# Decode attention and gated MLP on one core: query and down weights laid out in runs of rows, x loaded from ScalarE's queue

## The chip, the cores and the metric

The kernel runs on one NeuronCore of a Trainium2 chip. The metric is the device time of one execution in microseconds; lower is better. Three runs of the kernel before took 1316.83, 1316.87 and 1317.15 us, so its median is 1316.87 us.

## The reference

One decode step (one new token for each of 4 sequences) of a pre-norm transformer block: attention over a cache of 8192 keys and values for each of 32 heads, then a gated MLP. All inputs are bf16.

```python
B, D, H, Sk, Dh, F = 4, 512, 32, 8192, 128, 1792
def A(x):                                        # x: (4, 1, 512), layer-normed
    q = (x @ wq).reshape(B, 1, H, Dh)            # wq: (512, 4096)
    p = softmax(q . k_cache * Dh**-0.5)          # k_cache: (4, 32, 8192, 128)
    return (p . v_cache).reshape(B, 1, H*Dh) @ wo
def M(x):                                        # layer-normed
    return (sigmoid(x @ w_gate) * (x @ w_up)) @ w_down   # (512,1792), (512,1792), (1792,512)
h  = x + A(layernorm(x))
h2 = h + M(layernorm(h))
```

The two caches are 128 pairs (sequence, head) of 2 MB of keys and 2 MB of values: 537 MB. The weights are 4 MB each for `wq` and `wo` and 1.8 MB each for gate, up and down.

## The kernel before

Work is written out by hand, one list of instructions for each engine (`emit`) and DMAs put in the list of the engine that issues them (`prog.dma`); semaphores order them. All DMAs, x included, are issued by SyncE ("SPq" in the profile), strictly in the order of its list.

**Slots.** SBUF holds a ring of 8 slots of 2 MB (`KV`). Each K head, each V head and each of the three MLP weights takes the next slot (`take_slot`); the DMA that fills it waits until the slot's former holder has been used up. The order of loads is: x (L185), K head 0 in four pieces (L274), `wq` in four pieces of 1 MB (L295, `emit_wq`), K heads 1 and 2, then four pieces of `wo` (L302) between further K heads. From then on K and V heads alternate, V lagging K by 9 heads. `w_gate` stands before the last three V heads; the last V head comes in four pieces; `w_up` (both L290) and `w_down` in two pieces (L285) close the list. The first piece of `wo` overwrites `wq`'s buffer (`Wreg`), so SyncE waits there until the query projection is done.

**Start.** TensorE transposes x by four small matmuls (`f_xT`, L219), VectorE copies the result to `stx` and `sth`, a layer norm follows (`layernorm`, ending in `xnT`). TensorE transposes K head 0 (L360, evictions to `kTc` by ScalarE at L370 and VectorE at L372), then projects the query: 128 matmuls (L533), 32 for each quarter of the 512 rows of `wq`, each quarter waiting for its own DMA. In the stream a matmul loads its second operand into the array as weights (LDWEIGHTS, engine "PEld") and streams the third. Every weight operand of the kernel before is read with consecutive elements.

**Middle.** For each head: 64 transposes of K (L360), 16 score matmuls (L385), softmax for a group of 8 heads, and 16 matmuls with V (L469; for the last group 64 narrow ones a head, L481).

**End.** After the last piece of the last V head: project with `wo` (L498), second layer norm (L194 to L212, ending in `hnT`), gate and up products (L593, `glu_mm`, 56 matmuls each, to PSUM 128 hidden units at a time), sigmoid (L598), product `hhT` (L600), down product (L609, 56 matmuls; 28 for each half of `w_down`, each half waiting for its own DMA), add to the residual (L614), transpose (L616), copy (L618), store (L619).

Which hidden unit lies on which partition is fixed by the loads: before, partition p of tile t holds hidden unit 128 t + p for `w_down`, and `w_gate`/`w_up` columns are taken 128 in a row to match. In the same way partition p of chunk c holds row 128 c + p of `wq`, and `f_xT` puts x's element 128 c + p there.

Of the kernel before, what the change touches and what calls it, by code (L numbers as in the profile page):

```python
# [12 lines left out]
NTB = 4  # L13
NKT = 16
LAGH = 9
GH = 8


class _Prog:
# [27 lines left out]
    def emit(self, eng, fn, waits=(), incs=1):  # L47

        todo = self._waits(eng, waits)
        tok = self.token(eng, incs) if incs else None  # L50

        def run(e):
            for key, v in todo:
                e.wait_ge(self.sems[key], v)
            made = fn(e)
            made = made if isinstance(made, list) else [made]
            if incs:
                assert len(made) == incs
                for m in made:
                    m.then_inc(self.sems[eng], 1)  # L60

        self.ops[eng].append(run)
        return tok
# [14 lines left out]
def bass_sequential_preLN__mha_block_cached__glu_gated_glu__decode_kernel(  # L78
# [12 lines left out]
    B, _sq, D = A_x.shape  # L91
# [3 lines left out]
    NDC = D // 128  # L95
    NFT = F // 128
    R = S // 128
    NK = R // 4
    NH = B * H
    NG = NH // GH  # L100
    SCALE = float(DH) ** -0.5
# [3 lines left out]
    prog = _Prog()  # L105
    emit = prog.emit

    with ExitStack() as es:
        def SB(name, shape, dt):
            return es.enter_context(nc.sbuf_tensor(name, shape, dt))  # L110

        ident = SB("ident", [128, 128], BF16)
        identf = SB("identf", [128, 128], FP32)
        M8 = SB("M8", [128, GH], FP32)
        Gmat = SB("Gmat", [128, 128], FP32)
# [3 lines left out]
        x_bf = SB("x_bf", [B, D], BF16)  # L119
        stx = SB("stx", [128, 2 * NDC * B], FP32)  # L120
        sth = SB("sth", [128, 2 * NDC * B], FP32)
# [4 lines left out]
        q_all = SB("q_all", [128, NH], BF16)  # L126
        Lq = SB("Lq", [128, 2, GH * W], BF16)
        KV = SB("KV", [128, NSL, R * 128], BF16)
        kTc = SB("kTc", [128, NKT, 512], BF16)
        S_sb = SB("S_sb", [128, 512], FP32)  # L130
        E_sb = SB("E_sb", [128, 512], BF16)
        PT = SB("PT", [128, 2, NK * GH * 32], BF16)
        mpart = SB("mpart", [128, 1], FP32)
        mrow = SB("mrow", [1, GH], FP32)
        negmb = SB("negmb", [128, 1], FP32)
        sig = SB("sig", [128, 1], FP32)
        rsum = SB("rsum", [128, 1], FP32)
        O_sb = SB("O_sb", [128, 512], FP32)
        OT = SB("OT", [128, 2, GH], BF16)
        sg_sb = SB("sg_sb", [128, NFT * B], FP32)  # L140
# [5 lines left out]
        Wreg = SB("Wreg", [128, WREG], BF16)  # L146
        wq_v = Wreg[:, :].rearrange("p (c f) -> p c f", c=NDC)
# [7 lines left out]
        def in_slot(slot, inner):  # L155
            return bass.AP(raw(KV), slot * R * 128, [[KVROW, 128], *inner])
# [4 lines left out]
        bank = [PS[:, 512 * i:512 * (i + 1)] for i in range(8)]  # L161
        bankT = bank[0:4]
        SBK, OBK, XS, XO = 4, 5, 6, 7

        keys = ["sp", "act", "dve", "pool", "pe", "x", "out", "wg", "wu", "wd0", "wd1"]
        keys += [f"sl{i}" for i in range(NSL)] + [f"k0p{i}" for i in range(4)] + [f"vl{i}" for i in range(4)]
        keys += [f"wq{i}" for i in range(4)] + [f"wo{i}" for i in range(4)]
        for k in keys:
            prog.sems[k] = es.enter_context(nc.semaphore("s_" + k))

# [3 lines left out]
            out=ident[:, :], in_=ident[:, :], compare_op=ALU.not_equal, fill=1.0, base=0,  # L174
# [3 lines left out]
            out=identf[:, :], in_=identf[:, :], compare_op=ALU.not_equal, fill=1.0, base=0,  # L178
# [3 lines left out]
        t_rp0 = emit("pool", lambda e: e.memset(rowpad[:, :], 0.0))  # L182
        t_pt0 = emit("pool", lambda e: e.memset(PT[:, :, :], 0.0))

        t_x = prog.dma("sp", "x", lambda e: e.dma_start(x_bf[:, :], A_x.rearrange("b s d -> (b s) d")))  # L185


        def cols(t, c):
            return t[:, c:c + NDC * (B - 1) + 1:NDC]
# [26 lines left out]
        def f_xT(e):  # L216
            ins = None
            for c in range(NDC):
                ins = e.matmul(cols(bank[XO], c), x_bf[:, 128 * c:128 * (c + 1)], ident[0:B, 0:B],  # L219
                               start=True, stop=True)  # L220
            return ins
        t_xT = emit("pe", f_xT, [t_x, t_ident])
        t_xTc = emit("dve", lambda e: e.tensor_copy(stx[:, 0:NDC * B], bank[XO][:, 0:NDC * B]), [t_xT])
        t_h = emit("dve", lambda e: e.tensor_copy(sth[:, 0:NDC * B], bank[XO][:, 0:NDC * B]), [t_xT])
        t_xn, t_xst = layernorm(stx, t_xTc, 0, xnT, bank[XS], None)
        t_m8 = emit("dve", lambda e: e.tensor_reduce(
            M8[:, :], identf[:, :].rearrange("p (t i) -> p i t", i=GH), AX.X, ALU.max), [t_identf])
# [11 lines left out]
        t_wq = []  # L239
# [23 lines left out]
        def take_slot(job):  # L263
            i = n_alloc[0] % NSL
            w = freed(held_by[i])
            n_alloc[0] += 1
            held_by[i] = job
            slot_of[job] = i
            return i, w
# [9 lines left out]
        def emit_weight(kind):  # L279
            slot, w = take_slot((kind, 0))  # L280
            if kind == "wd":
                wd_v = in_slot(slot, [[D, NFT], [1, D]])
                src = B_w_down.rearrange("(t p) f -> p t f", p=128)
                half = NFT // 2
                t_w[kind] = (wd_v, [prog.dma("sp", f"wd{i}", lambda e, i=i: e.dma_start(  # L285
                    wd_v[:, half * i:half * (i + 1), :], src[:, half * i:half * (i + 1), :]), w) for i in range(2)])
                return
            view = in_slot(slot, [[F, NDC], [1, F]])
            src = (B_w_gate if kind == "wg" else B_w_up).rearrange("(c p) f -> p c f", p=128)
            t_w[kind] = (view, prog.dma("sp", kind, lambda e: e.dma_start(view, src), w))  # L290

        def emit_wq():
            src = A_wq.rearrange("(c p) f -> p c f", p=128)
            for c in range(NDC):
                t_wq.append(prog.dma("sp", f"wq{c}", lambda e, c=c: e.dma_start(wq_v[:, c, :], src[:, c, :])))  # L295

        t_wo = []
        t_qproj = []
# [7 lines left out]
        for n in range(NH):  # L306
            order.append((4 * n, 0, "k", n))
            order.append((4 * (n + LAGH), 1, "v", n))
        order.sort()
# [218 lines left out]
        def q_projection():  # L528
            for c in range(NDC):
                def f(e, c=c):  # L530
                    ins = None
                    for h in range(H):
                        ins = e.matmul(bank[XO][:, B * h:B * (h + 1)], wq_v[:, c, h * 128:(h + 1) * 128],  # L533
                                       cols(xnT, c), start=(c == 0 and h == 0),
                                       stop=(c == NDC - 1), skip_group_check=True)
                    return ins
                t = emit("pe", f, [t_wq[c], t_xn, t_xTc])
            t_qproj.append(t)
            st_["q"] = st_["xo"] = emit("dve", lambda e: e.tensor_copy(q_all[:, :], bank[XO][:, 0:NH]), [t])
            q_windows(0)  # L540
            q_windows(1)

        def q_windows(g):
            dst = Lq[:, g % 2, 31:31 + W * (GH - 1) + 1:W]
            t_lq[g] = emit("dve", lambda e: e.tensor_copy(dst, q_all[:, GH * g:GH * (g + 1)]),  # L545
                           [st_["q"], t_lq0, t_score.get(32 * (g - 1) - 1)])


        for u in range(4 * (NH + LAGH)):
            n, s = u // 4, u % 4  # L550
# [10 lines left out]
            for su in todo:  # L561
                if su < 4 * NH:
                    scores(su)
                    if su % 32 == 31:
                        if 2 <= su // 32 + 2 < NG:
                            q_windows(su // 32 + 2)
                        for d, fn in softmax(su // 32):
                            chain.append((4 * u + d, fn))
            vu = u - 4 * LAGH
            if vu >= 0:  # L570
# [17 lines left out]
        def glu_mm(wv, bk):  # L588
            def f(e):
                ins = None  # L590
                for t in range(NFT):
                    for c in range(NDC):
                        ins = e.matmul(bk[:, B * t:B * (t + 1)], wv[:, c, 128 * t:128 * (t + 1)],  # L593
                                       cols(hnT, c), start=(c == 0), stop=(c == NDC - 1))
                return ins
            return f
# [3 lines left out]
        t_hh = emit("dve", lambda e: e.tensor_tensor(hhT[:, :], sg_sb[:, :], bank[SBK][:, 0:NF], ALU.mult), [t_sg, t_u])  # L600

        wd_v, t_wd = t_w["wd"]
        half = NFT // 2
        for i in range(2):
            def f_down(e, i=i):
                ins = None
                for t in range(half * i, half * (i + 1)):
                    for c in range(NDC):
                        ins = e.matmul(cols(bank[OBK], c), wd_v[:, t, 128 * c:128 * (c + 1)],  # L609
                                       hhT[:, B * t:B * (t + 1)], start=(t == 0 and c == 0),  # L610
                                       stop=(t == NFT - 1), skip_group_check=True)
                return ins
            t_d = emit("pe", f_down, [t_hh, t_wd[i], t_ot])
# [3 lines left out]
                                            start=True, stop=True), [t_h2])  # L617
# [59 lines left out]
```

## Time and profile before

| | |
|---|---|
| median of 3 runs | 1316.87 us |
| span of the profiled execution (first to last instruction) | 1315.5 us |
| around the span (median less span) | 1.4 us |
| TensorE matmul busy (PE) | 1016.4 us, 77% |
| TensorE weight loads (PEld) | 671.9 us, 51% |
| VectorE (DVE) | 721.1 us, 55% |
| ScalarE (ACT) | 608.7 us, 46% |
| bytes by DMA | 552.68 MB, 420 GB/s over the span |
| mean granted TensorE clock | 0.845 |

The page gives no time of its own for the profiled execution beside its span, so the median of the runs stands in for it. Busy shares are averages over the span; a DMA share of 9 tenths or more means that the 16 DMA engines had packets in flight nearly always. In the chain of waits "SPq" is SyncE issuing DMAs and "DMA" is the time from the end of an issue to the landing. TensorE, where it waits for data, idles "<-DMA".

### The profile page before, as it was taken

The page shows a single profiled execution, that of the slowest core. Times are in us where ns is not written, and L with a number is a line of the kernel's source. Part 1 is how long each engine was busy: PE and PEld are TensorE (multiplying, and loading weights), DVE is VectorE, ACT ScalarE, POOL GpSimd, SP SyncE. Part 2 cuts the span into 40 slices and gives each one's busy share as a digit, 9 for nine tenths or more (in the row PEclk, how much of TensorE's full clock was granted, in tenths as well). Part 3 has the DMA queues.
Part 4 walks back from the last instruction along what each step waited for, and adds up shares of the span by engine and source line. Part 5 has one row for each costly group of instructions (what it writes and reads, how often), then busy time and mean ns, then how long its engine had stood idle before and what let it go on. Part 6 is the DMA issues. An engine that isn't in the chain of part 4 may idle for free.

```text
span 1315.5 us, 29564 instructions
## 1 busy us (share of the span) xinstructions
PE 1016.4 (77%) x13385; PEld 671.9 (51%) x13385; DVE 721.1 (55%) x1210; ACT 608.7 (46%) x1095; POOL 9.0 (1%) x11
## 2 busy tenths in 40 slices
PE   6887877877788787887788778788887878778764
PEld 5654544545455454554455445455554545545443
DVE  5774655556555565555556456555555656556520
ACT  3664544545444454444445445454444545445420
POOL 2000000000000000000000000000000000000000
PEclk8988888888888888788888888888788888888865
DMA  9999999999999999999999999999999999999996
GB/s 381 415 427 426 427 427 427 425 428 425 428 425 426 427 425 428 424 427 426 427 426 426 426 428 424 427 425 428 427 424 426 426 428 425 426 427 428 425 411 245
DMA packets 45510, 552.68 MB, mean 420 GB/s; under 512 B 4420, under 2 KB 10312, under 8 KB 12360
## 3 DMA queue, kind: packets, MB, share of 16 engines
q1 hardware_dynamic: 45384, 550.79, 99.0%
q8 instruction: 105, 1.72, 0.5%
q14 instruction: 21, 0.17, 0.0%
HBM read 550.77 MB, written 0.00 MB: 419 GB/s over the span
## 4 chain that ended last, share of the span: by engine, by line
DMA 81%; PE 16%; SPq 2%; ACT 0%; issue 0%; DVE 0%
DMA KV<-in_A_v_cache_dram 76%; PE PS L360 10%; PE PS L385 3%; PE PS L469 3%; DMA KV<-in_B_w_down_dram 2%; DMA KV<-in_A_k_cache_dram 1%; SPq L277 1%; DMA Wreg<-in_A_wq_dram 1%; SPq L302 0%; SPq L295 0%; ACT kTc L370 0%; SPq L274 0%; ACT L422 0%; PE PS L533 0%; PE PS L481 0%
## 5 line engine op out<-in xcount | busy, mean ns | idle before, releaser
L372 DVE CAST kTc<-PS 128x512 bf16<-128x512 f32 x1024 | 676.1, 692 | 484.4 <-PE PS L360 481.6
L370 ACT ACTIVATE kTc<-PS 128x512 bf16<-128x512 f32 x1024 | 573.4, 595 | 648.2 <-PE PS L360 646.2
L360 PEld LDWEIGHTS PS<-ident,KV 128*128 128x128 bf16 x8192 | 547.5, 109 | 252.3 <-ACT kTc L370 135.7
L360 PE MATMUL PS<-ident,KV 128*128 128x128 bf16 x8192 | 654.7, 240 | 12.8 <-DMA KV<-in_A_k_cache_dram 10.4
L469 PE MATMUL PS<-KV,PT 128*32 128x512 bf16 x1920 | 216.8, 442 | 242.2 <-DMA KV<-in_A_v_cache_dram 242.2
L385 PE MATMUL PS<-kTc,Lq 128*32 128x512 bf16 x2048 | 227.1, 435 | 1.1 <-DVE Lq L545 0.6
L469 PEld LDWEIGHTS PS<-KV,PT 128*32 128x32 bf16 x1920 | 52.4, 99 | 273.9 <-DMA KV<-in_A_v_cache_dram 273.6
L385 PEld LDWEIGHTS PS<-kTc,Lq 128*32 128x32 bf16 x2048 | 53.5, 95 | 64.6 <-issue 19.1
L481 PE MATMUL PS<-PT,KV 128*128 128x1 bf16 x512 | 14.9, 165 | 18.0 <-DMA KV<-in_A_v_cache_dram 15.4
L481 PEld LDWEIGHTS PS<-PT,KV 128*128 128x128 bf16 x512 | 14.3, 104 | 18.6 <-DMA KV<-in_A_v_cache_dram 15.9
L516 PE MATMUL PS<-selq,O_sb 128*128 128x8 f32 x120 | 16.7, 266 | 7.1 <-ACT O_sb L508 7.1
L516 PEld LDWEIGHTS PS<-selq,O_sb 128*128 128x128 f32 x120 | 15.3, 200 | 10.0 <-ACT O_sb L508 10.0
L409 DVE TENSOR_REDUCE mrow<-PS 1x8 f32<-1x128 f32 x16 | 4.5, 279 | 29.2 <-PE PS L405 29.2
L205 ACT ACTIVATE lnw<-lnw 128x4 f32<-128x4 f32 x2 | 0.4, 205 | 38.9 <-DVE lnw L202 38.9
L581 DVE CAST OT<-PS 128x8 bf16<-128x8 f32 x1 | 0.2, 167 | 32.6 <-PE PS L481 32.6
L521 DVE CAST OT<-PS 128x8 bf16<-128x8 f32 x15 | 2.5, 167 | 19.5 <-PE PS L516 19.5
L422 ACT ACTIVATE E_sb<-S_sb,negmb 128x512 bf16<-128x512 f32 x16 | 11.6, 722 | 3.1 <-DVE negmb L420 2.6
L400 DVE TENSOR_REDUCE mpart<-S_sb 128x1 f32<-128x512 f32 x16 | 11.0, 686 | 3.1 <-ACT S_sb L398 1.5
L508 ACT ACTIVATE O_sb<-PS 128x512 f32<-128x512 f32 x15 | 9.0, 597 | 6.3 <-PE PS L469 6.3
L446 DVE CAST PT<-PS 128x512 bf16<-128x512 f32 x16 | 10.9, 682 | 0.7 <-PE PS L438 0.7
L398 ACT ACTIVATE S_sb<-PS 128x512 f32<-128x512 f32 x16 | 9.6, 597 | 1.2 <-PE PS L385 1.1
L405 PE MATMUL PS<-identf,mpart 128*1 128x128 f32 x32 | 7.5, 325 | 2.4 <-DVE mpart L400 2.4
(67 smaller groups left out, 119.5 us busy)
## 6 DMA issues: line engine op xcount, KB each, us to landing
KV<-in_A_k_cache_dram SPq DMA_DIRECT2D x127, 2048.0 KB, 28.7
KV<-in_A_v_cache_dram SPq DMA_DIRECT2D x127, 2048.0 KB, 33.1
Wreg<-in_A_wq_dram SPq DMA_DIRECT2D x4, 1024.0 KB, 11.7
Wreg<-in_A_wo_dram SPq DMA_DIRECT2D x4, 1024.0 KB, 14.1
KV<-in_A_k_cache_dram SPq DMA_DIRECT2D x4, 512.0 KB, 5.7
KV<-in_A_v_cache_dram SPq DMA_DIRECT2D x4, 512.0 KB, 26.6
KV<-in_B_w_gate_dram SPq DMA_DIRECT2D x1, 1792.0 KB, 28.1
KV<-in_B_w_up_dram SPq DMA_DIRECT2D x1, 1792.0 KB, 26.4
```

The lines of the kernel that those rows point to most:

```text
L277: done[n] = [prog.dma("sp", f"sl{slot}", lambda e: e.dma_start(KV[:, slot, :], src), w)] * 4
L360: ins = e.matmul(bankT[g % NTB][:, 128 * i:128 * (i + 1)], KV[:, slot, r * 128:(r + 1) * 128], ident[:, :], start=True, stop=True)
L370: t_copy[g] = emit("act", lambda e: e.activation(kTc[:, ks, :], bankT[g % NTB][:, :], ACT.Copy), w)
L372: t_copy[g] = emit("dve", lambda e: e.tensor_copy(kTc[:, ks, :], bankT[g % NTB][:, :]), w)
L385: mms.append(e.matmul(PS[32 * j:32 * (j + 1), 512 * SBK:512 * (SBK + 1)], Lq[:, g % 2, off:off + 32], kTc[:, (n * NK + k) % NKT, :], start ...
L398: t_sev[g] = emit("act", lambda e: e.activation(S_sb[:, :], bank[SBK], ACT.Copy), [t_score[32 * g + 31], st_.get("exp")])
L400: t_mx = emit("dve", lambda e: e.tensor_reduce(mpart[:, :], S_sb[:, :], AX.X, ALU.max), [t_sev[g], st_.get("p1")])
L422: box["a2"] = emit("act", lambda e: e.activation(E_sb[:, :], S_sb[:, :], ACT.Exp, bias=negmb[:, 0:1], scale=SCALE, accum_out=sig[:, 0:1]), ...
L446: st_["xs"] = t_ptc[g] = emit("dve", lambda e: e.tensor_copy(dst, src), [t, t_pt0, t_pvg.get(g - 2)])
L469: mms.append(e.matmul(PS[32 * j:32 * (j + 1), 512 * OBK:512 * (OBK + 1)], PT[:, pb, o:o + 32], KV[:, slot, 512 * k:512 * (k + 1)], start=f ...
L481: ins = e.matmul(bank[OBK][:, i:i + 1], KV[:, slot, 128 * r:128 * (r + 1)], PT[:, pb, o:o + 1], start=(r == 0), stop=(r == R - 1))
L516: ins = e.matmul(bank[XO][:, 0:GH], O_sb[:, 128 * q:128 * (q + 1)], selq[:, q:q + 29:4], start=(q == 0), stop=(q == 3))
```

## The change

The 512 rows of `wq` go to partitions in runs: partition p gets rows 4p to 4p+3, one run of 32 KB, and one DMA loads them all. The query projection waits for that one DMA in every quarter. To match, `f_xT` takes every fourth element of x for the layer norm's copy; it keeps the former order for the residual `sth`, so it has 8 matmuls for 4. `w_down`'s 1792 rows go to partitions in runs of 14 rows (14 KB), in three DMAs of 8, 4 and 2 rows a partition, with the down product split likewise (32, 16 and 8 matmuls). To match, the gate and up products take as weights every 14th column of `w_gate`/`w_up` (28 bytes from one to the next). x is issued from ScalarE's list, ahead of all its other work.

```diff
+WDT = (0, 8, 12, 14)
...
-        t_x = prog.dma("sp", "x", lambda e: e.dma_start(x_bf[:, :], A_x.rearrange("b s d -> (b s) d")))
+        t_x = prog.dma("act", "x", lambda e: e.dma_start(x_bf[:, :], A_x.rearrange("b s d -> (b s) d")))
...
             for c in range(NDC):
-                ins = e.matmul(cols(bank[XO], c), x_bf[:, 128 * c:128 * (c + 1)], ident[0:B, 0:B],
-                               start=True, stop=True)
+                e.matmul(cols(bank[XO], c), x_bf[:, c:c + NDC * 127 + 1:NDC], ident[0:B, 0:B],
+                         start=True, stop=True)
+            for c in range(NDC):
+                ins = e.matmul(cols(bank[XO][:, NDC * B:2 * NDC * B], c), x_bf[:, 128 * c:128 * (c + 1)],
+                               ident[0:B, 0:B], start=True, stop=True)
             return ins
...
-        t_h = emit("dve", lambda e: e.tensor_copy(sth[:, 0:NDC * B], bank[XO][:, 0:NDC * B]), [t_xT])
+        t_h = emit("dve", lambda e: e.tensor_copy(sth[:, 0:NDC * B], bank[XO][:, NDC * B:2 * NDC * B]), [t_xT])
...
-                src = B_w_down.rearrange("(t p) f -> p t f", p=128)
-                half = NFT // 2
+                src = B_w_down.rearrange("(p t) f -> p t f", p=128)
                 t_w[kind] = (wd_v, [prog.dma("sp", f"wd{i}", lambda e, i=i: e.dma_start(
-                    wd_v[:, half * i:half * (i + 1), :], src[:, half * i:half * (i + 1), :]), w) for i in range(2)])
+                    wd_v[:, WDT[i]:WDT[i + 1], :], src[:, WDT[i]:WDT[i + 1], :]), w) for i in range(len(WDT) - 1)])
...
         def emit_wq():
-            src = A_wq.rearrange("(c p) f -> p c f", p=128)
-            for c in range(NDC):
-                t_wq.append(prog.dma("sp", f"wq{c}", lambda e, c=c: e.dma_start(wq_v[:, c, :], src[:, c, :])))
+            src = A_wq.rearrange("(p c) f -> p (c f)", p=128)
+            t_wq.append(prog.dma("sp", "wq", lambda e: e.dma_start(Wreg[:, :], src)))
...
-                t = emit("pe", f, [t_wq[c], t_xn, t_xTc])
+                t = emit("pe", f, [t_wq[0], t_xn, t_xTc, t_h])
...
-                        ins = e.matmul(bk[:, B * t:B * (t + 1)], wv[:, c, 128 * t:128 * (t + 1)],
+                        ins = e.matmul(bk[:, B * t:B * (t + 1)], wv[:, c, t:t + NFT * 127 + 1:NFT],
                                        cols(hnT, c), start=(c == 0), stop=(c == NDC - 1))
...
-        half = NFT // 2
-        for i in range(2):
+        for i in range(len(WDT) - 1):
             def f_down(e, i=i):
                 ins = None
-                for t in range(half * i, half * (i + 1)):
+                for t in range(WDT[i], WDT[i + 1]):
```

The rest of the diff renames semaphores (one for `wq`, a third for `w_down`).

More of the change, by code (lines that the diff above doesn't have):

```diff
@@ L163, in bass_sequential_preLN__mha_block_cached__glu_gated_glu__decode_kernel @@
         SBK, OBK, XS, XO = 4, 5, 6, 7
-        keys = ["sp", "act", "dve", "pool", "pe", "x", "out", "wg", "wu", "wd0", "wd1"]
+        keys = ["sp", "act", "dve", "pool", "pe", "x", "out", "wg", "wu", "wd0", "wd1", "wd2"]
         keys += [f"sl{i}" for i in range(NSL)] + [f"k0p{i}" for i in range(4)] + [f"vl{i}" for i in range(4)]
-        keys += [f"wq{i}" for i in range(4)] + [f"wo{i}" for i in range(4)]
+        keys += ["wq"] + [f"wo{i}" for i in range(4)]
         for k in keys:
```

## The prediction

> **What bounds the kernel now.** I read the page's slices and the chain of waits first. They say that the transfers set the pace.
>
> ```profile
> DMA  9999999999999999999999999999999999999996
> q1 hardware_dynamic: 45384, 550.79, 99.0%
> q8 instruction: 105, 1.72, 0.5%
> DMA 81%; PE 16%; SPq 2%; ACT 0%; issue 0%; DVE 0%
> ```
>
> The DMA engines are full in 39 of 40 slices, and 81% of the chain that ended last is DMA. Nothing that TensorE does in the middle moves the end. The change touches only the first 25 us and the last 30, so I read those by stage: windows, TensorE's timeline and the end of the chain.
>
> ```profile
> 0.00:5.00 5.00, 0.86 (x6) 0.68 (x6) 1.56 (x11) 1.49 (x2) 4.10 (x11) 1.00 0.51 147
> 20.00:25.00 5.00, 2.48 (x44) 1.23 (x44) 0.55 (x3) 0.00 (x0) 0.00 (x0) 0.50 0.99 423
> 1306.20:1308.20 2.00, 2.00 (x80) 2.00 (x79) 0.00 (x0) 0.90 (x2) 0.00 (x0) 0.50 0.54 180
> 1308.20:1310.20 2.00, 1.62 (x61) 1.54 (x59) 0.21 (x1) 0.00 (x0) 0.00 (x0) 0.50 0.54 187
> ```
>
> Last column GB/s, before it the DMA share. From 1306 to 1310 half of the engines' capacity moves bytes: about 8 of 16 run late, and the end waits for these. (The instruction queue's 105 packets take about 1.06 us each in the packet records, 14 us apiece if eight engines carry them, which fits.) A late engine never idles, so a microsecond saved anywhere in its stream is a microsecond at the last landing.
>
> ```profile
> 1302.23 0.59 PE L481 MATMUL PS<-PT,KV 128*128 128x1 bf16 x16 [0.67 <-DMA KV<-in_A_v_cache_dram]
> 1306.06 3.15 PE L593 MATMUL PS<-hnT,KV 128*128 128x4 bf16 x112 [1.31 <-DVE hnT L212]
> 1309.58 0.91 PE L609 MATMUL PS<-hhT,KV 128*128 128x4 bf16 x28 [0.38 <-DVE hhT L600]
> 1311.89 0.91 PE L609 MATMUL PS<-hhT,KV 128*128 128x4 bf16 x28 [1.40 <-DMA KV<-in_B_w_down_dram]
> ```
>
> Two strands meet in the last line. One is DMA: the second half of w_down lands at 1311.84 and 28 matmuls follow. The other is compute: last V piece (1302.23), layer norm, gate and up, first half of down, done at 1310.49. It is only 1.40 us ahead. That is all the cover that the gate and up products have.
>
> **Part by part.** Sums are made on the span, 1315.5 us; the median, 1316.87, lies 1.4 us above, and I carry that over.
>
> *x on ScalarE's queue.* SyncE's stream begins with x: issue at 0.74, K at 1.15. The first slice shows idle engines (share 0.51), so all loads start 0.41 us sooner: **-0.41 us** on every landing, zero at worst. On ScalarE the issue (0.36 us) stands ahead of a 1.28 us table load from 0.73; its first use is at 4.48, so it is hidden (0.4 us of layer norm if not, which the query projection, waiting for wq, covers). Four more matmuls in f_xT are about 0.1 us, hidden before the first K piece (5.46).
>
> *wq in one load.* By the trace's packet records an 8 KB packet takes 309 ns and a 16 KB one 611. A late engine has 32 of 8 KB, 9.89 us; eight of 32 KB are 9.78 by the 16 KB rate: **-0.1 us** (between -0.3 and +0.3, as no packet of 32 KB is in the trace). The projection loses its head start. Before, 64 of 128 matmuls ran at 14.65 and the last 32 after the landing at 20.33. Now all 128 follow a landing at 19.8: at 1.74 us for 64 they end at 23.3, not 21.40. Behind that wait SyncE holds the first wo piece, all further K heads and V; on TensorE the scores of head 0 and the transposes of K1 wait 1.9 us. Cover: K1 and K2 are already queued. By 21.4 there are 10.5 MB issued; the windows move 9.2 MB by 25.0, so bytes last to 28.2. wo issued at 23.3 and starting 1.6 us later (x: issue 0.74, landing 2.29) arrives 3.3 us in time. Cost **0**; without that cover up to 1.9.
>
> *w_down in 14 KB runs.* Before, a late engine has 112 packets of 1 KB at 44 to 47 ns, 4.9 to 5.3 us. After: 8 of 8 KB (309), 8 of 4 KB (159), 8 of 2 KB (between 46 and 92, say 85), 4.4 us: **-0.6 us** (-0.5 to -0.9). With the two gains before, the last piece lands at 1311.84 - 1.1 = 1310.7. It then needs 8 matmuls, not 28: 0.3 for 0.92 us, **-0.6 us**. So the DMA strand alone gives **-1.7 us**.
>
> *Gate and up with weights 28 bytes apart.* This is the price. Before, 112 loads and matmuls take 3.15 us, 27.3 ns a pair. No weight load in the trace steps over elements, so I bound it. Below: no cost, 27.3 ns. Above: VectorE reading SBUF with a step.
>
> ```profile
> L226 DVE TENSOR_REDUCE M<-identf x1: 377/377/377, 5.0 to 5.0; 128x8 f32<-128x128 f32 x1
> L228 DVE TENSOR_REDUCE selq<-identf x1: 361/361/361, 5.3 to 5.3; 128x32 f32<-128x128 f32 x1
> L196 DVE TENSOR_REDUCE lnr<-sth x1: 186/186/186, 1303.9 to 1303.9; 128x8 f32<-128x32 f32 x1
> L400 DVE TENSOR_REDUCE mpart<-S_sb x16: 685/686/687, 73.1 to 1261.1; 128x1 f32<-128x512 f32 x16
> ```
>
> Contiguous reduces (L196, L400): 500 ns for 480 more elements, 1.04 ns each on 153 fixed. With steps of 32 and 128 bytes: (369 - 153) / 128 = 1.69 ns. A step costs 1.63 times there. Were all 128 columns fetched singly at that pace, a load would take 216 ns. But 128 columns now come in 27.3 ns, 0.21 each, so several are fetched at once, and I apply the ratio: 27.3 x 1.63 = **44 ns** (43 to 46 by the two rows singly; 54 if four columns come at once, each at 1.69 ns: a load of 32 columns, L385, has the record of one of 128, 95 and 96 ns). Between 44 and 216 lies a load reduced to one column a turn of TensorE at half clock, as in the transposes:
>
> ```profile
> 1206.55 1.82 PE PS L360 x16
> ```
>
> That is 114 ns for 128 columns.
>
> The Trainium skill ("SBUF — State Buffer", section "Door 1: The DMA port swizzle") speaks against this edit: SBUF delivers full bandwidth only if at least two accesses hit the same 16-byte line, so bf16 may step up to 8 elements, and 14 is beyond. The two VectorE rows agree that stepping costs. The page names no price; taken as a doubling it would make 54.6 ns, an estimate, and the end 1317.9.
>
> Compute strand after: the last V piece lands 0.5 sooner, so gate starts at 1305.55. With L ns a load it runs 0.112 L + 0.09 us, 0.37 us more to the first down matmul, 56 matmuls of 29.7 ns with their start 1.75 us. Its end is 1307.76 + 0.112 L, against 1312.81 now: **-5.05 + 0.112 L us**. At 44 ns: 1312.7, **-0.1 us**, and later than the DMA strand (1311.1). The gain is eaten and the end waits for TensorE, not for w_down. Break-even is at 45 ns.
>
> **Forecast, chance 0.29:** the step costs about 1.6 times; 1316.87 - 0.1 = **1316.8 us**. Its own range, loads of 43 to 54 ns: 1316.6 to 1317.9.
>
> **Rivals.**
> - *The step is free (0.21).* The DMA strand decides: -1.7 us, **1315.2**. For it: the load's reads may have slack at half clock (window rows: clock 0.50), since a load record is 104 ns there and 96 at full clock (L593, L533), so its spacing is not all reading. Against: the VectorE rows.
> - *The fetch falls back to one column a turn (0.27).* **Slower:** -5.05 + 0.112 x 114 = +7.7 us, **1324.6**. Place: the 112 loads of L593, with 1.40 us of cover. It decides from 69 ns a load (+2.6 us, 0.2%). For it: 128 columns 28 bytes apart touch 128 places where 256 contiguous bytes stand now, so whatever fetches them together may not. Against: VectorE lost 1.6 times, not four.
> - *Each at VectorE's stepped pace (0.11).* 216 ns: +19.1, **1336**. Against it, TensorE's reads are already five times denser than VectorE's.
> - *The queue runs dry behind the later projection (0.06).* Up to 1.9 us at 28 us on top of the forecast, **1318.7**; against it the 3.3 us of cover.
> - *x does not start K sooner, or the big packets give nothing* moves each case by at most 0.5 us and is inside the ranges.
> The remaining 0.06 is for what I do not see.
>
> **How the numbers follow.** The range 1314.8 to 1324.9 holds the forecast, the free step, the dry queue and the one-column case; the 216 ns case and the unseen, 0.17, lie outside. A change within 0.2%, 2.6 us, is about what a measurement of this kernel can tell from no change. Slower: 0.27 + 0.11 and, with the forecast's upper tail past 69 ns and the unseen, 0.06: 0.44. Faster by 2.6 us needs a free step and 0.9 us more than I can find: 0.09. The rest, 0.47, is same. The three signs are close because one unseen number, the price of a stepped weight load, decides between them.
>
> **What would show it.** L593's span against 3.15 us (5.1 by forecast, 3.1 free, 12.9 singly); what L609's last group waits for: w_down if the step is free, hhT with no DMA idle if not. K's first issue at 0.74; L533 in one group of 128 ending near 23.3; about 420 GB/s kept from 25 to 35; the last w_down landing near 1310.7. Wrong if L593 is unmoved and the end still is, or if a middle slice drops below 420 GB/s.

## The result and the profile after

The changed kernel takes 1319.14 us (median of 20 runs) against 1316.89 us (20 runs): ratio 1.0016, 95% interval 1.001 to 1.0022. It is 2.25 us slower. That is within the 0.2% (2.6 us) that the prediction counts as no change, but clear of the runs' noise, and on the other side of the 0.1 us gain that was forecast.

The profiled execution spans 1317.4 us, 1.9 us more than before. The page of the kernel after, slices, queues and the chain of waits:

```profile
DMA  9999999999999999999999999999999999999995
q1 hardware_dynamic: 43552, 550.79, 98.8%
q8 instruction: 105, 1.72, 0.5%
DMA 80%; PE 17%; SPq 2%; DVE 0%; issue 0%; ACT 0%; DVEq 0%
```

Transfers still fill 39 slices, with 1832 packets fewer. One per cent of the chain has gone from DMA to TensorE, and w_down is no longer among the chain's lines. TensorE's timeline at the end of the kernel after (start, length, line; in brackets the idle time before and what ended it):

```profile
1301.98 0.59 PE L483 MATMUL PS<-PT,KV 128*128 128x1 bf16 x16 [0.75 <-DMA KV<-in_A_v_cache_dram]
1305.80 6.88 PE L595 MATMUL PS<-hnT,KV 128*128 128x4 bf16 x112 [1.31 <-DVE hnT L213]
1313.07 1.66 PE L610 MATMUL PS<-hhT,KV 128*128 128x4 bf16 x56 [0.38 <-DVE hhT L602]
1314.98 0.28 PE L617 MATMUL PS<-ident,h2T 128*16 128x128 bf16 x1 [0.26 <-DVE h2T L615]
```

The last V piece arrives 0.25 us sooner than before (1301.98 for 1302.23) and gate and up start 0.26 us sooner. Then these 112 matmuls take 6.88 us instead of 3.15. The down product, formerly in two groups with a wait for w_down between them, runs as one group of 56 that waits for hhT only. Its end is 1314.73, against 1312.80 before.

Two windows of the kernel after (last columns: granted clock, DMA share, GB/s) show the other side:

```profile
1308.20:1310.20 2.00, 2.00 (x36) 2.00 (x36) 0.00 (x0) 0.22 (x1) 0.00 (x0) 0.50 0.37 146
1310.20:1312.20 2.00, 2.00 (x37) 2.00 (x35) 0.00 (x0) 0.00 (x0) 0.00 (x0) 0.50 0.00 1
```

From 1310.2 on hardly a byte moves. The three loads of `w_down` in the kernel after (first and last start of an issue, then the times from an issue to its landing):

```profile
L288 SPq DMA_DIRECT2D KV<-in_B_w_down_dram x3: 1026/1032/11763, 1281.9 to 1294.8; - x3
DMA to landing us min/median/max: 15.9/16.3/26.9
```

The last one was issued at 1294.8 and landed 15.9 us later, at 1310.7; before, the last one landed at 1311.84. The transfers ended 1.1 us earlier, and nobody could use it: TensorE had 1.9 us of gate and up products still to do (they end at 1312.68).

At the start, SyncE's list of the kernel after and the projection:

```profile
0.74 1.82 SPq L278 DMA_DIRECT2D KV<-in_A_k_cache_dram  x4
18.90 3.57 PE L535 MATMUL PS<-xnT,Wreg 128*128 128x4 bf16 x128 [4.44 <-DMA Wreg<-in_A_wq_dram]
22.50 0.38 SPq L304 DMA_DIRECT2D Wreg<-in_A_wo_dram  x1
```

K is issued at 0.74 instead of 1.15. The projection is one run of 128 matmuls, and `wo` is issued 1.1 us later than before (22.50 for 21.42). From 20 to 35 us the windows give 416 GB/s, before 419: hardly any loss, at most 0.1 us of transfer.

### The profile page after: what moved, and what is told of

Same layout as the page of the kernel before. It is cut to its first block, busy times and chain, and to the rows that moved or that the text cites. A ratio compares the mean times of both kernels' runs of the same rounds, so it can differ in the third digit from the quotient of the medians.

```text
span 1317.4 us, 29570 instructions
## 1 busy us (share of the span) xinstructions
PE 1011.3 (77%) x13389; PEld 669.0 (51%) x13389; DVE 719.8 (55%) x1210; ACT 607.2 (46%) x1095; POOL 9.0 (1%) x11
## 4 chain that ended last, share of the span: by engine, by line
DMA 80%; PE 17%; SPq 2%; DVE 0%; issue 0%; ACT 0%; DVEq 0%
DMA KV<-in_A_v_cache_dram 77%; PE PS L362 9%; PE PS L471 3%; PE PS L387 3%; DMA KV<-in_A_k_cache_dram 1%; DMA Wreg<-in_A_wq_dram 1%; SPq L281 1%; SPq L278 1%; PE PS L595 1%; SPq L304 0%; PE PS L535 0%; PE PS L483 0%; PE PS L518 0%; PE PS L610 0%; DVE kTc L374 0%
## 5 line engine op out<-in xcount | busy, mean ns | idle before, releaser
L362 PEld LDWEIGHTS PS<-ident,KV 128*128 128x128 bf16 x8192 | 540.9, 108 | 254.3 <-ACT kTc L372 133.3
L362 PE MATMUL PS<-ident,KV 128*128 128x128 bf16 x8192 | 647.5, 239 | 16.0 <-DMA KV<-in_A_k_cache_dram 13.1
L523 DVE CAST OT<-PS 128x8 bf16<-128x8 f32 x15 | 2.5, 167 | 19.8 <-PE PS L518 19.8
```

The source lines that it names most:

```text
L362: ins = e.matmul(bankT[g % NTB][:, 128 * i:128 * (i + 1)], KV[:, slot, r * 128:(r + 1) * 128], ident[:, :], start=True, stop=True)
```

## Experiments

The theory: the longer gate and up products, whose weights lie 28 bytes apart, are the whole loss. The rival: the start loses it, through the later projection and the single load of `wq`. A second question was what the price of a stepped weight load follows. The edits shown in experiments 1 and 4 are against the kernel before, the others against the kernel after; what only follows from them (names of semaphores, matching transposes of x) is left out.

### 1. The price of a step by itself

Blocks of 64 matmuls added behind the last copy of the kernel before, one for each step, here written once with `s` for the step:

```diff
+pw = lambda o, s: in_slot(slot_of[('wg', 0)], [[1, 8192]])[:, o:o + 127 * s + 1:s]
+emit('pe', lambda e: [e.matmul(po(i), pw(i % 8, s), cols(hnT, 0), start=True, stop=True) for i in range(64)][-1], pb)
```

> The kernel before with 13 blocks of 64 weight loads (each with a 4-column matmul) added behind its last copy, columns 1, 2, 4, 6, 7, 8, 9, 10, 12, 14, 16, 28 and 56 elements apart, then four blocks of 32 (steps 1, 8, 14, 28) each right behind 24 matmuls of 512 columns that raise the clock. Results of the blocks are not read. Theory A (a price per 16-byte place touched): 27 ns a pair at step 1, a rise with the step up to 8 elements, flat at 61 ns from 8 on. Theory B (any step costs the same, because the loads no longer take neighbouring elements together): 27 ns at step 1, 61 ns at every other step. Theory C (the Trainium skill's SBUF page, up to 8 elements free): 27 ns up to step 8, 61 ns from 9 on. If reads are hidden at half clock, the blocks behind the long matmuls cost more at step 14 than 61 ns; if reads keep the array's clock, less.

Seen once, without repeats (1387.62 us with all blocks). TensorE's timeline of this kernel, steps 1, 2, 4, 6, 7, 8 and 9, 64 matmuls to a line:

```profile
1313.51 1.87 PE L624 MATMUL PS<-hnT,KV 128*128 128x4 bf16 x64 [0.37 <-DVE o_sb L618]
1315.23 1.85 PE L625 MATMUL PS<-hnT,KV 128*128 128x4 bf16 x64
1316.94 2.29 PE L626 MATMUL PS<-hnT,KV 128*128 128x4 bf16 x64
1319.09 3.16 PE L627 MATMUL PS<-hnT,KV 128*128 128x4 bf16 x64
1322.11 3.58 PE L628 MATMUL PS<-hnT,KV 128*128 128x4 bf16 x64
1325.55 3.98 PE L629 MATMUL PS<-hnT,KV 128*128 128x4 bf16 x64
1329.40 3.98 PE L630 MATMUL PS<-hnT,KV 128*128 128x4 bf16 x64
```

From one start to the next, divided by 64:

| step (elements) | 1 | 2 | 4 | 6 | 7 | 8 | 9 | 10 | 12 | 14 | 16 | 28 | 56 |
|---|---|---|---|---|---|---|---|---|---|---|---|---|---|
| 16-byte places touched | 16 | 32 | 64 | 96 | 112 | 128 | 128 | 128 | 128 | 128 | 128 | 128 | 128 |
| ns for a load with its matmul | 27 | 27 | 34 | 47 | 54 | 60 | 60 | 58 | 60 | 60 | 62 | 63 | 60 |

The places are counted for a block that starts at the edge of one; the starts vary by up to 7 elements. The DMA share was 0.04 or less while these blocks ran, so transfers into SBUF are not what makes the price.

Theory A holds: from 64 places on, each 16 more cost 6.4 to 6.8 ns, and beyond one place for each column there is no further rise (58 to 63 ns). Theory B falls with step 2, which is free. Theory C falls too: the Trainium skill ("SBUF — State Buffer", section "Door 1: The DMA port swizzle") lets bf16 step 8 elements for free, and here step 8 already pays the full price. Its other statement, that at least two accesses must hit the same line, fits better, but not quite: at step 4 (two to a line) 7 of the 33 ns are already paid.

Behind 24 long matmuls the clock was 1.00 instead of 0.50. Steps 8 and 14 at that clock:

```profile
1369.29 2.04 PE L640 MATMUL PS<-hnT,KV 128*128 128x4 bf16 x32
1371.19 5.34 PE L641 MATMUL PS<-KV,ident 128*128 128x512 bf16 x24
1376.37 2.03 PE L642 MATMUL PS<-hnT,KV 128*128 128x4 bf16 x32
1378.26 5.34 PE L643 MATMUL PS<-KV,ident 128*128 128x512 bf16 x24
```

From one start to the next these are 1.90 and 1.89 us for 32 pairs, 59 ns each, as at half clock. The two other blocks at that clock took 25 ns a pair at step 1 and some 62 at step 28. So at these steps the price does not follow TensorE's clock; neither expectation on the clock (more, or less) came true.

### 2. The kernel after without the step

```diff
-                        ins = e.matmul(bk[:, B * t:B * (t + 1)], wv[:, c, t:t + NFT * 127 + 1:NFT],
+                        ins = e.matmul(bk[:, B * t:B * (t + 1)], wv[:, c, 128 * t:128 * (t + 1)],
```

> The kernel after with the gate and up products reading 128 neighbouring columns again (one edit; hidden units are then paired with other rows of w_down, amounts of work and all loads unchanged). Theory (the stepped weight loads are the whole loss): L595 falls from 6.88 to 3.15 us, the down product ends near 1311.0, the time is 1315.0, ratio 0.9986 to the kernel before. Rival (the loss comes from the start, from the later query projection and the one load of wq): 1318 to 1319.

This kernel multiplies hidden units with other rows of `w_down`, so it does the same amount of work but does not compute the block.

Measured: 1315.62 us, ratio 0.9989 (0.998 to 0.9998). One slice in one line turns 2.25 us of loss into 1.4 us of gain. The timeline of this kernel's end:

```profile
1305.89 3.15 PE L595 MATMUL PS<-hnT,KV 128*128 128x4 bf16 x112 [1.32 <-DVE hnT L213]
1309.41 1.44 PE L610 MATMUL PS<-hhT,KV 128*128 128x4 bf16 x48 [0.38 <-DVE hhT L602]
1311.02 0.38 PE L610 MATMUL PS<-hhT,KV 128*128 128x4 bf16 x8 [0.16 <-DMA KV<-in_B_w_down_dram]
```

L595 is back at 3.15 us, and the last 8 matmuls wait for `w_down` again and start at 1311.02. The rival (1318 to 1319) falls.

### 3. The w_down part alone

x and `wq` as in the kernel before, everything else as after (the transposes of x stay eight, in the former order):

```diff
-        t_x = prog.dma("act", "x", lambda e: e.dma_start(x_bf[:, :], A_x.rearrange("b s d -> (b s) d")))
+        t_x = prog.dma("sp", "x", lambda e: e.dma_start(x_bf[:, :], A_x.rearrange("b s d -> (b s) d")))
...
-            src = A_wq.rearrange("(p c) f -> p (c f)", p=128)
+            src = A_wq.rearrange("(c p) f -> p c f", p=128)
```

> Only the w_down part of the change (runs of 14 rows, three loads, stepped gate and up weights); x and wq as before. Theory: the last V piece lands as before, gate starts at 1306.06, 6.88 us, down ends 1314.97, +2.2 us: 1319.1 to 1319.4. Rival (the start is to blame): at or below 1316.9.

Measured: 1319.48 us, ratio 1.0018 (1.0009 to 1.0027). The part that holds the stepped loads carries the whole loss; L595's counterpart started at 1306.11 and took 6.88 us.

### 4. x alone and wq alone

```diff
-        t_x = prog.dma("sp", "x", lambda e: e.dma_start(x_bf[:, :], A_x.rearrange("b s d -> (b s) d")))
+        t_x = prog.dma("act", "x", lambda e: e.dma_start(x_bf[:, :], A_x.rearrange("b s d -> (b s) d")))
```

> Only x moved to ScalarE's queue. Theory: every load starts 0.4 us sooner and the late engines never idle, so the end is 0.4 us sooner, 1316.6. Rival (the gain is lost before the end, in waits for slots): 1317.0.

Measured: 1316.57 us against 1316.97, ratio 0.9997 (0.9988 to 1.0006). The size of the step, 0.4 us, is the one expected, but the interval holds no change too. Its first window has 181 GB/s for 147 before.

```diff
-            src = A_wq.rearrange("(c p) f -> p c f", p=128)
-            for c in range(NDC):
-                t_wq.append(prog.dma("sp", f"wq{c}", lambda e, c=c: e.dma_start(wq_v[:, c, :], src[:, c, :])))
+            src = A_wq.rearrange("(p c) f -> p (c f)", p=128)
+            t_wq.append(prog.dma("sp", "wq", lambda e: e.dma_start(Wreg[:, :], src)))
```

> Only the query weights in one load (with the transposes of x that go with it). Theory: the projection ends 1 to 2 us later, covered by two queued K heads, so the time is the same within 0.2 us, 1316.8 to 1317.0. Rival (the queue runs dry behind the projection): up to 1.9 us more, 1318 to 1319, with a window between 20 and 35 us below 390 GB/s.

Measured: 1316.79 us, ratio 0.9999 (0.999 to 1.0008). The projection ran from 19.24 for 3.58 us and `wo` was issued at 22.85. One window is low, from 25 to 30:

```profile
20.00:25.00 5.00, 4.29 (x118) 3.03 (x115) 0.55 (x3) 0.00 (x0) 0.00 (x0) 0.50 1.01 429
25.00:30.00 5.00, 4.81 (x62) 3.82 (x63) 3.45 (x6) 3.28 (x6) 0.00 (x0) 0.83 0.97 384
30.00:35.00 5.00, 5.00 (x80) 3.90 (x79) 4.82 (x8) 4.01 (x9) 0.00 (x0) 1.00 1.08 445
```

It is below the 390 GB/s that I named as the rival's mark, but its neighbours make up for it: 419 GB/s from 20 to 35, the same as in the kernel before, where the 25 to 30 window has 397. The mark was badly chosen, and the time decides: the queue does not run dry.

### 5. Smaller steps: bands of rows

Bands of 8, 4 and 2 rows a partition, so that packets stay as in the kernel after and the weights lie 8, 4 and 2 elements apart:

```diff
-                src = B_w_down.rearrange("(p t) f -> p t f", p=128)
+                src = [B_w_down[128 * WDT[i]:128 * WDT[i + 1], :].rearrange("(p t) f -> p t f", p=128)
+                       for i in range(len(WDT) - 1)]
...
+            i = max(j for j in range(len(WDT) - 1) if WDT[j] <= t)
+            r, o = WDT[i + 1] - WDT[i], 128 * WDT[i] + t - WDT[i]
+            return slice(o, o + 127 * r + 1, r)
```

> The kernel after with w_down's rows laid out in three bands, runs of 8, 4 and 2 rows in 1024, 512 and 256 rows, so that packets stay 8, 4 and 2 KB and the gate and up weights lie 8, 4 and 2 elements apart instead of 14. By theory A: 64 loads at 61 ns and 48 at 27 to 40, L595 5.3 to 5.8 us, 1317.0 to 1317.7. By theory B 6.9 us, 1319.1. By theory C 3.15 us, 1315.0. If the start is to blame: 1319 whatever L595 does.

Measured: 1317.58 us, ratio 1.0005 (0.9996 to 1.0014); the products took 5.53 us, within the range of theory A and between the values of theories B and C. With the table of experiment 1 it is 64 x 60 + 32 x 34 + 16 x 27 ns = 5.4 us. By that sum a step of 8 saves nothing against 14, and the whole saving comes from the steps of 4 and 2.

Seven bands of 256 rows, a run of 2 rows to a partition in each:

```diff
-                src = B_w_down.rearrange("(p t) f -> p t f", p=128)
+                src = B_w_down.rearrange("(b p t) f -> p b (t f)", p=128, t=2)
...
-                        ins = e.matmul(bk[:, B * t:B * (t + 1)], wv[:, c, t:t + NFT * 127 + 1:NFT],
+                        ins = e.matmul(bk[:, B * t:B * (t + 1)], wv[:, c, 256 * (t // 2) + t % 2:256 * (t // 2) + t % 2 + 255:2],
```

> The kernel after with w_down in seven bands of 256 rows, a run of 2 rows (2 KB) to a partition in each, still in three loads of 8, 4 and 2 rows; gate and up weights then lie 2 elements apart. If the price is one for each 16-byte place, 128 columns 2 apart touch 32 places and a pair stays at 27 ns (L595 3.1 us); w_down takes 56 packets of 84 ns in a late engine, 4.7 us for 4.4, 0.3 us behind the contiguous run's: 1315.9, ratio 0.9991. If any step costs, L595 is 6.9 us and the time 1319.

Measured: **1315.58 us**, ratio 0.999 (0.9981 to 0.9999), the lowest median here, with `w_down`'s rows and hidden units paired as the reference has them: 1.4 us faster than the kernel before and 3.6 us faster than the kernel after. The intervals do not separate it from experiments 2 and 6. Its end:

```profile
1305.46 3.15 PE L596 MATMUL PS<-hnT,KV 128*128 128x4 bf16 x112 [1.31 <-DVE hnT L213]
1308.99 1.02 PE L611 MATMUL PS<-hhT,KV 128*128 128x4 bf16 x32 [0.38 <-DVE hhT L603]
1310.17 1.00 PE L611 MATMUL PS<-hhT,KV 128*128 128x4 bf16 x24 [0.16 <-DMA KV<-in_B_w_down_dram]
```

A step of 2 costs nothing: 3.15 us.

### 6. The short last piece without larger packets

```diff
-                src = B_w_down.rearrange("(p t) f -> p t f", p=128)
+                src = B_w_down.rearrange("(t p) f -> p t f", p=128)
...
-                        ins = e.matmul(bk[:, B * t:B * (t + 1)], wv[:, c, t:t + NFT * 127 + 1:NFT],
+                        ins = e.matmul(bk[:, B * t:B * (t + 1)], wv[:, c, 128 * t:128 * (t + 1)],
```

> The kernel after with w_down's rows in the order of the kernel before (packets of 1 KB, gate and up weights neighbouring), loaded in three DMAs of 8, 4 and 2 tiles. It keeps the short last product, and loses the large packets: 112 packets at 46 ns, 5.1 us for 4.4, so 0.7 us later than the contiguous run of the first set: 1316.3. If packet size is worth nothing at the end: 1315.6.

Measured: 1315.88 us, ratio 0.9992 (0.9983 to 1.0001). It lies 0.3 us above the versions with larger packets (1315.58 and 1315.62), less than the 0.7 that the packet durations gave, and the intervals don't separate them. The profiles say more. From the start of the last V piece's matmuls to the landing of the last `w_down` piece it took 9.3 us here (1301.78 to 1311.05). It took 8.8 to 8.9 us in the four kernels with packets of 8, 4 and 2 KB (the kernel after, experiments 2 and 3, and the first of experiment 5). By these, larger packets are worth some 0.4 to 0.5 us at the landing. That is one profile a kernel, and the same stretch differed by 0.2 us between two kernels with equal `w_down` loads (9.6 in the kernel before, 9.4 with x alone moved).

## Why the prediction was wrong

The path was right. The gain of the transfers was eaten by the stepped weight loads, the compute strand took over the end, and `w_down` was no longer waited for, all as in the forecast case. The step that failed is the size of one term: **27.3 x 1.63 = 44 ns a load**. The runs show 61 ns (6.88 us for 112; 60 ns by itself). The prediction's own formula, -5.05 + 0.112 L, gives +1.8 us at 61 ns, where the span of the profiled executions grew by 1.9 and the median of the times by 2.25. With 44 ns it gave -0.1. Part of the gap between 1.9 and 2.25 lies in the profile that the prediction worked on: its span of 1315.5 us is on the long side for the kernel before, whose runs in the experiments have 1314.7 to 1315.6. The time around the span, taken as 1.4 us, was 1.8 in the profiled execution of the kernel after (1319.16 us with a span of 1317.4).

The term was wrong in its form too. I took the ratio by which VectorE slows when it steps, although VectorE's elements come 1.04 ns apart and the load's columns 0.21 ns. Contiguous, 128 columns touch 16 places of 16 bytes; 28 bytes apart they touch 128. Eight times the places cost 2.2 times the time: in the table of experiment 1, up to 32 places cost no more than the 27 ns of a contiguous pair. The upper end of the forecast's own range, 54 ns, was nearer; the estimate of 54.6 ns from a doubling likewise. The rival of one column a turn (114 ns, 1324.6 us) gave the right reason, 128 places where the contiguous load has 16, but was nearly twice too dear: it tied the fetch to TensorE's clock, and the price at step 14 is the same at clock 0.50 and 1.00. The free step (1315.2 us) did not happen, but experiment 2 shows what it would have given, 1315.6, and experiment 5 got there with a step of 2.

The other terms:

- *x*: the first K issue at 0.74 as predicted, 0.4 us of gain alone (not resolved by its interval).
- *wq*: the landing came sooner than predicted (18.85 for 19.8), for a reason that the runs do not show; the projection ended at 22.47 for 23.3, and the cover held. The 0.1 us is below what the runs resolve.
- *w_down*: its last piece landed at 1310.7, as predicted, but with some luck. The last V piece came 0.25 us sooner for 0.5, and the stretch from there to the landing shrank by 0.85 us for 0.6. In experiment 2, where the piece was waited for again, it landed at 1311.0, and the DMA strand alone gave -1.4 us for the predicted -1.7.
- *compute strand*: the start of gate and up came 0.26 us sooner, not 0.5. The profiles of experiment 2 and of the two kernels of experiment 5, with the same edits at the start, have it at 1305.89, 1305.50 and 1305.46, so this moves by some 0.4 us between profiles.
- *the rest of the strand*: 0.39 us from gate and up to the first down matmul and 1.66 for 56, where 0.37 and 1.75 were taken.

## What to carry to other kernels

A layout that gives each partition longer runs for the DMA can put a step into whatever reads the other side of the contraction; here a run of r rows made the weights of the product before lie r elements apart. Count the 16-byte places a weight load touches, and choose the run so that it stays where the load is not yet the limit: runs of 2 rows kept the gain, runs of 14, or bands with runs of 8, lost it. Where two strands meet at the end, read how much the shorter one may grow before an edit that shortens the longer: here it was 1.4 us, and the edit lengthened it by 3.7.

## What the runs showed of the hardware

A load of 128 bf16 weights with a 4-column matmul took 27 ns up to a step of 2 elements, 34 at 4, 47 at 6, 60 at 8, and 58 to 63 from 9 to 56. These are readings at granted clock 0.50, seen in one execution; the kernels with steps of 14, of 8, 4 and 2, and of 2 agree with them (6.88, 5.53 and 3.15 us for 112). At granted clock 1.00 a step of 8 or 14 took 59 ns. That a step beyond 16 bytes adds nothing stood in theory A; that the granted clock does not matter there, no theory had.
